# Attention before a mixture of experts: an exponential's low half moved to GpSimd, v's low half in one step, gains spread by a product, a new instruction order

## The chip, the cores and the metric

The kernel runs on one core of one Trainium2 chip. The metric is the device time of one execution in microseconds (us); lower is better. The core has five instruction streams that run side by side and wait for each other through semaphores: TensorE (products into PSUM), VectorE, ScalarE, GpSimd, and SP, which here only issues DMAs. Each executes its own instructions strictly in order.

## The reference

Attention with normalised queries and keys for 8 batches of 12 heads, 448 positions and 64 columns a head, and behind it a layer of 8 experts over the 3584 tokens. Each expert takes 448 tokens, chosen greedily by the logits.

```python
def rmsnorm(x, g):
    rms = np.sqrt(np.mean(x * x, axis=-1, keepdims=True) + 1e-06)
    return x / rms * g
q_n, k_n = (rmsnorm(q, g_q), rmsnorm(k, g_k))
scores = np.matmul(q_n, k_n.transpose(0, 1, 3, 2)) / np.sqrt(q.shape[-1])
attn = np.exp(scores - np.max(scores, axis=-1, keepdims=True))
attn = attn / (np.sum(attn, axis=-1, keepdims=True) + 1e-09)
x = np.matmul(attn, v)                  # then to 3584 tokens of 768
logits = x @ w_gate                     # greedy choice, 448 tokens an expert
for e in range(8):
    out[mask_e] = np.maximum(x[mask_e] @ w1[e], 0.0) @ w2[e]
```

## The kernel before

The kernel keeps single precision by splitting most operands into two 16-bit halves (high and low) and adding three products: high by high, high by low, low by high.

**Tiling.** The 96 heads are worked in 24 groups of four (two pairs). The 448 positions of a pair of heads are seven blocks for each group, so there are 168 blocks d of 128 x 896 scores. Per group: q and k are loaded (lines 222 and 230), squared on ScalarE (`square`), summed on VectorE (`sumsq`, line 286), normalised on GpSimd (k, line 321) and ScalarE (q, line 318), multiplied by `gg` = g_q g_k on GpSimd (`gain`, line 346), split into halves (`hi` on ScalarE, `lo` on GpSimd, lines 351 and 354) and turned by DMA transposes on SP (`transpose`, line 363). For the first two groups (`EARLY`) TensorE does the turning (line 376). Then for each block:

- `max_score` (line 473): a rough product into the one PSUM tile of ring `pm`; `max_reduce` (line 482): VectorE takes the row maxima out of it.
- `scores` (lines 504 and 506): the full product; `exp` (line 512): ScalarE writes the exponentials in single precision.
- `split` (line 528): the low half of an exponential, the full value less its top 16 bits, on GpSimd for the blocks in `LO_POOL` and on VectorE for the others. Blocks in `WIDE` are not split; they are multiplied in single precision (line 547).
- `av` (lines 547 to 557): products with v into a PSUM tile of ring `po` (two buffers).

`MIX` names one of two kinds for every group: nine groups are "4" (blocks 0, 2, 4, 6 wide, low halves of 1, 3, 5 on GpSimd) and fifteen are "2" (blocks 0 and 4 wide; of 1, 2, 3, 5, 6 the low half of block 2 is made by VectorE, the other four by GpSimd). v is loaded into `vraw`, and its halves are made for the position columns that are not wide: `v_hi` on ScalarE (line 440) and `v_lo` on VectorE (line 444). `halves_v` yields the parts: one of 512 columns in a "4" group, two (512 and 256 columns) in a "2" group.

Behind every pair, `x_norm`, `x_hi`, `x_lo` (lines 579 to 602) divide by the sums and write x in halves; line 601 and 602 set the `po` tile free. Per batch (three groups), x is stored (`x_store`, lines 616 and 620), turned by two DMA transposes on SP (`x_dma_turn`, line 609, 24 and 18 blocks) and multiplied by the gate weights (`gate`, lines 658 to 666, into a `po` tile). `Router.early` does the first step of the choice for the first six batches on VectorE.

**Setting up.** `gain_loads` reads g_q and g_k by two DMAs of GpSimd that repeat the row for all 128 partitions (line 143); `gate_loads` reads the gate weights by five DMAs on SP (lines 146 and 150); `gains` multiplies g_q by g_k on VectorE (line 178).

**Order.** Nothing is scheduled while the kernel is built: `plan` lists 2247 tasks, each with its engine, an estimated time (table `US`) and its dependencies, and the string `ORDER` (two characters a task) is the order in which they are issued. `Plan.run` checks that it holds to the dependencies and issues them; each engine then executes its own in that order. The estimates are used for finding such a string only, not when the kernel is built.

After attention the router and the eight experts run (`Router`, `Experts`; lines 864 to 1800), with weights streamed in by SP.

Of the kernel before, what the change touches and what calls it, by code (L numbers as in the profile page):

```python
# [26 lines left out]
F32 = mybir.dt.float32  # L27
# [4 lines left out]
OP = mybir.AluOpType  # L32
# [57 lines left out]
class Attention:  # L90
# [19 lines left out]
    LO_POOL = {"4": (1, 3, 5), "2": (1, 3, 5, 6), "0": (1, 3, 5)}  # L110
    MIX = "444" + 6 * "422" + "222"

    def __init__(self, ctx, tc, q, k, v, g_q, g_k, w_gate, xd, logits, router):
# [13 lines left out]
        gq = c.tile([128, 64], F32, name="gq")  # L127
        gk = c.tile([128, 64], F32, name="gk")
# [31 lines left out]
        def eps():  # L160
            for t in self.sq:
                nc.gpsimd.memset(t[:, :, 64:65], 64e-6)

# [13 lines left out]
        def gains():  # L177
            nc.vector.tensor_tensor(self.gg, gq, gk, op=OP.mult)
# [149 lines left out]
    def engine(self, e, g, a=None):  # L328
        some = self.FIRST[g] if g < len(self.FIRST) else self.TAIL if g >= self.NG - 2 else {}
        return some.get(f"{e}{a}", some.get(e, self.ENG[e]))  # L330
# [99 lines left out]
    def halves_v(self, g):  # L430
# [11 lines left out]
    def v_lo(self, g):  # L442
        for r, h, l in self.halves_v(g):
            self.nc.vector.scalar_tensor_tensor(l, r, self.VS, h, op0=OP.mult, op1=OP.subtract)  # L444
# [159 lines left out]
    def x_dma_turn(self, b, part):  # L604
# [3 lines left out]
        s = slice(24 * part, 24 + 18 * part)  # L608
# [93 lines left out]
    def gate_sum(self, b):  # L702
# [5 lines left out]
    US = dict(small=0.22, rootP=1.19, rootD=0.6, copyA=0.95, sumsq=1.09, normP=1.69, normA=2.1,  # L708
              normD=1.08, gainP=2.09, gainD=1.08, loP=1.89, loD=1.08, turn=1.95, trm=1.16, rows=1.05, loadS=0.66,
              loadA=0.6, loadP=1.0, max=0.2, reduce=1.092, score=0.765, wide=0.248, narrow=0.092,  # L710
              exp=0.917, splitD=1.08, splitP=1.68, xn=0.63, xhi=0.605, xlo=0.68, gate=0.11, early=8.0, xturn=0.4, xtdA0=0.81,
# [4 lines left out]
    def plan(self):  # L716
# [11 lines left out]
        add("gl", "P", 1.32, gain_loads, make="gg32", move=(1.5, 0.4))  # L728
        add("gg", "D", 0.15, gains, after=["gg32"], make="gg")
# [4 lines left out]
        for g in range(self.NG):  # L734
# [18 lines left out]
            else:  # L753
# [25 lines left out]
                for i in range(2):  # L779
                    add("tr" + "hl"[i], "S", US["turn"], self.transpose, g, i, after=[("hl"[i], g, n) for n in "kq"], make=("kq", g, i),  # L780
# [1074 lines left out]
```

## Time and profile before

| | |
|---|---|
| time, median of 3 runs | 998.96 us (994.08 to 999.85) |
| the profiled execution | 998.89 us, span 997.1 us |
| busy in the span: TensorE / VectorE / ScalarE / GpSimd | 92% / 69% / 53% / 43% |
| mean granted TensorE clock | 0.959 of full |
| moved by DMA | 157.78 MB |

The page gives such shares for the whole span; since attention and the experts load the engines differently, the views below are taken by stretches. "L482" is line 482 of the kernel, `out<-in` names the tiles, and an arrow behind idle time names what ended it. TensorE's clock has two levels, 1.2 and 2.4 GHz; a granted clock of 0.50 is the lower.

### The profile page before, as it was taken

To read this page: it belongs to the slowest core of one execution; us is meant where nothing else is said; L and a number is where in the kernel's file an instruction comes from. 1 tells how busy PE (TensorE), PEld (TensorE's weight loads), DVE (VectorE), ACT (ScalarE), POOL (GpSimd) and SP (SyncE) were. 2 spreads that over 40 slices of the span, in tenths; PEclk is the share of its full clock that TensorE was granted. 3 is DMA by queue.
4 is the path that set the end of the run, shared out by engine and by line. 5 is a ranking of instruction groups with operands and counts; after the bars stand their busy time and mean duration, and the time that the engine had idled before them with its cause. 6 is when DMAs were issued, how large, how long until landed. Compare 5 with 4: busy or idle time off the path is not lost.

```text
span 997.1 us, 24885 instructions
## 1 busy us (share of the span) xinstructions
PE 921.2 (92%) x10285; PEld 592.7 (59%) x10286; DVE 691.0 (69%) x1518; ACT 531.8 (53%) x1055; POOL 432.6 (43%) x420
## 2 busy tenths in 40 slices
PE   1889989899899999899869999999999999999996
PEld 1466666666677666667746655556555565555553
DVE  4979998878868788776488777778686758334010
ACT  4879887779778987755405243424242424334111
POOL 5779886877877977854210110311111112020101
PEclk9789999899989999989959999999999999999998
DMA  7286597878889876566236483949493919663101
GB/s 167 79 164 140 128 186 159 190 166 174 173 192 214 157 154 137 112 157 123 69 103 208 141 256 120 278 155 264 146 258 105 300 60 300 220 161 117 40 16 40
DMA packets 263841, 157.78 MB, mean 158 GB/s; under 512 B 189456, under 2 KB 250896, under 8 KB 262704
## 3 DMA queue, kind: packets, MB, share of 16 engines
q1 hardware_dynamic: 258224, 133.65, 55.6%
q0 software_dynamic: 4672, 22.09, 6.6%
q8 instruction: 80, 1.31, 0.5%
q10 hardware_dynamic: 832, 0.46, 0.2%
q14 instruction: 33, 0.27, 0.1%
HBM read 94.49 MB, written 22.02 MB: 117 GB/s over the span
## 4 chain that ended last, share of the span: by engine, by line
issue 33%; PE 16%; POOL 5%; DVE 3%; ACT 1%; POOLq 0%; DVEq 0%; ACTq 0%
PE ph L1638 6%; PE py L1655 3%; POOL out_dram L1671 2%; POOL rows L1576 2%; PE po L547 2%; PE psc L504 2%; PE po L553 1%; PE po L557 1%; PE po L555 1%; PE psc L506 0%; PE rp L1239 0%; PE pm L473 0%; ACT qn L318 0%; DVE vs L444 0%; POOL spacer L1670 0%
## 5 line engine op out<-in xcount | busy, mean ns | idle before, releaser
L482 DVE TENSOR_REDUCE mx<-pm 128x2 f32<-128x896 f32 x162 | 176.2, 1088 | 55.2 <-PE pm L473 54.3
L1638 PE MATMUL ph<-xt,w1h 128*128 128x448 f16 (+2 forms) x804 | 209.7, 344 | 1.0 <-DVE xt L1597 0.5
L547 PE MATMUL po<-v,e 128*128 128x65 f32 (+1 forms) x1056 | 180.0, 285 | 1.6 <-ACT e L512 1.4
L528 POOL TENSOR_TENSOR pl<-e 128x896 f16<-128x896 f32 x87 | 152.0, 1751 | 57.1 <-ACT e L512 56.9
L512 ACT ACTIVATE e<-psc 128x896 f32<-128x896 f32 x168 | 149.1, 912 | 46.6 <-PE psc L506 42.1
L1671 POOL DMA_INDIRECT out_dram<-y,idx x32 | 33.2, 1036 | 311.5 <-ACT y L1657 238.9
L547 PEld LDWEIGHTS po<-v,e 128*128 128x128 f32 (+1 forms) x1056 | 136.9, 182 | 39.3 <-issue 33.7
L1638 PE MATMUL ph<-xt,w1l 128*128 128x448 f16 (+2 forms) x402 | 136.8, 344 | 0.0
L504 PE MATMUL psc<-kq 64*128 64x448 f16 (+1 forms) x1152 | 131.4, 370 | 5.3 <-ACT e L512 4.2
L555 PE MATMUL po<-vs,e 128*128 128x64 f16 (+1 forms) x1008 | 133.3, 197 | 0.0
L553 PE MATMUL po<-vs,e 128*128 128x65 f16 (+1 forms) x1008 | 132.9, 198 | 0.0
L557 PE MATMUL po<-vs,pl 128*128 128x65 f16 (+1 forms) x1008 | 131.9, 196 | 0.0
L1655 PE MATMUL py<-w2h,hh 128*128 128x384 f16 x384 | 125.0, 326 | 0.0
L1655 PE MATMUL py<-w2h,hl 128*128 128x384 f16 x384 | 125.0, 326 | 0.0
L1655 PE MATMUL py<-w2l,hh 128*128 128x384 f16 x384 | 125.0, 325 | 0.0
L1628 ACT ACTIVATE hh<-ph 128x448 f16<-128x448 f32 x64 | 34.8, 543 | 146.4 <-PE ph L1638 129.6
L553 PEld LDWEIGHTS <-e 128*128 128x128 bf16 (+1 forms) x1008 | 112.1, 126 | 0.0
L1638 PEld LDWEIGHTS <-w1h 128*128 128x128 f16 x804 | 74.1, 97 | 61.3 <-issue 1.5
L1655 PEld LDWEIGHTS <-hh 128*128 128x128 f16 x768 | 73.6, 97 | 45.8
L1657 ACT ACTIVATE y<-py 128x384 f32<-128x384 f32 x48 | 23.5, 490 | 133.4 <-PE py L1655 102.2
L557 PEld LDWEIGHTS <-pl 128*128 128x128 f16 (+1 forms) x1008 | 88.7, 103 | 0.0
L1630 DVE SCALAR_TENSOR_TENSOR hl<-ph,hh 128x448 f16<-128x448 f32 x64 | 39.3, 619 | 71.2 <-ACT hh L1628 71.1
(272 smaller groups left out, 1835.3 us busy)
## 6 DMA issues: line engine op xcount, KB each, us to landing
stage<-in_moe_w_dram SPq DMA_DIRECT2D x64, 768.0 KB
vraw<-in_v_dram SPq DMA_DIRECT2D x24, 384.0 KB
xd<-xa SPq DMA_DIRECT2D x8, 1152.0 KB
qkraw<-in_q_dram SPq DMA_DIRECT2D x11, 768.0 KB
qkraw<-in_k_dram SPq DMA_DIRECT2D x11, 768.0 KB
vraw<-in_v_dram SPq DMA_DIRECT2D x48, 32.0 KB
xd<-xa SPq DMA_DIRECT2D x16, 96.0 KB
qkraw<-in_q_dram SPq DMA_DIRECT2D x22, 64.0 KB
```

The lines of the kernel that those rows point to most:

```text
L482: self.nc.vector.tensor_reduce(m, p[r, :, :448], axis=AX.X, op=OP.max)
L504: mm(o, k[r, mine], q[r, all_], start=i == 0, stop=False)
L512: self.nc.scalar.activation(e, p[:, :, :448], AF.Exp, scale=scale)
L528: eng.tensor_tensor(l, self.T["e", d], self.T["ph", d], op=OP.subtract)
L547: nc.tensor.matmul(out, self.T["e", d][:, h, q0:q0 + m], self.v32[g % 2][:, 2 * h + a, wide.index(b % 4)], start=first, stop=last)
L553: nc.tensor.matmul(out, e[:, h, q0:q0 + m], vh, start=first, stop=False)
L555: nc.tensor.matmul(out[:, :64], e[:, h, q0:q0 + m], vl[:, :64], start=False, stop=False)
L557: nc.tensor.matmul(out, l[:, h, q0:q0 + m], vh, start=False, stop=last)
L1630: self.later(0.6, lambda: nc.vector.scalar_tensor_tensor(hl, whole, 0.0, hh, op0=OP.max, op1=OP.subtract), k, 3.5, f)
L1638: nc.tensor.matmul(p, a, b[:, o], start=st, stop=sp)
L1655: nc.tensor.matmul(p, a[:, f, s], b[:, f, o], start=st, stop=sp)
L1671: st = nc.gpsimd.indirect_dma_start(out=self.out, out_offset=bass.IndirectOffsetOnAxis(ap=self.router.idx[k][:n, c:c + 1], axis=0), in_=y[ ...
```

## The change

Five things are changed, all in attention.

1. `LO_POOL["2"]` gains block 2: in the fifteen "2" groups all five low halves are made by GpSimd. VectorE makes none any more.
2. `halves_v` yields one part of all 1024 columns in a "2" group (the wide quarter with them, which nobody reads), so `v_hi` and `v_lo` are one instruction there. A "4" group keeps its one step of 512.
3. g_q and g_k are loaded as single rows, by SP and by ScalarE's queue. VectorE multiplies the rows, a product of TensorE with a row of ones spreads the result over 128 partitions of a `po` tile, and VectorE copies it into `gg`.
4. `x_dma_turn` turns x in four pieces (12, 12, 12 and 6 blocks) in place of two.
5. `ORDER` is another string (2262 tasks). Estimates in `US` and in `plan` that served to find it are changed too.

Read from the two strings: the gate-weight loads are task 6 before and 460 after; `Router.early` is task 2041 of 2247 before and 2189 of 2262 after. SP begins with load 0 of q, the gate weights, loads 2, 1 and 3 of q before; with loads 0, 1, 2 of q, g_q, load 3 of q after. ScalarE's queue begins with four loads of k before; with three, g_k and the fourth after.

```diff
-    LO_POOL = {"4": (1, 3, 5), "2": (1, 3, 5, 6), "0": (1, 3, 5)}
+    LO_POOL = {"4": (1, 3, 5), "2": (1, 2, 3, 5, 6), "0": (1, 3, 5)}
...
-        gq = c.tile([128, 64], F32, name="gq")
-        gk = c.tile([128, 64], F32, name="gk")
+        gq = c.tile([1, 64], F32, name="gq")
+        gk = c.tile([1, 64], F32, name="gk")
+        one = c.tile([1, 128], F32, name="one")
...
-        def gain_loads():
-            for t, src in ((gq, g_q), (gk, g_k)):
-                nc.gpsimd.dma_start(t, bass.AP(tensor=src.tensor, offset=src.offset, ap=[[0, 128], [1, 64]]))
+        def gain_loads(i):
+            eng, t, src = ((nc.sync, gq, g_q), (nc.scalar, gk, g_k))[i]
+            eng.dma_start(t, bass.AP(tensor=src.tensor, offset=src.offset, ap=[[64, 1], [1, 64]]))
...
         def gains():
-            nc.vector.tensor_tensor(self.gg, gq, gk, op=OP.mult)
+            nc.vector.tensor_tensor(gq, gq, gk, op=OP.mult)
+            p = self.po_tile()[:, :64]
+            nc.tensor.matmul(p, one, gq, start=True, stop=True)
+            nc.vector.tensor_copy(self.gg, p)
...
         js = [j for j in range(4) if j not in self.wide_of(g)]
-        for part in (js[:3:2], js[1:2], js[3:]) if len(js) == 3 else (js,):
-            if part:
-                yield self.heads(r, part), *(self.heads(vs[:, i], part)[..., :64] for i in range(2))
+        js = js if len(js) == 2 else [0, 1, 2, 3]
+        if len(js) == 4:
+            yield r, vs[:, 0, :, :64], vs[:, 1, :, :64]
+        else:
+            yield self.heads(r, js), *(self.heads(vs[:, i], js)[..., :64] for i in range(2))
...
-        s = slice(24 * part, 24 + 18 * part)
+        s = slice(12 * part, min(42, 12 * part + 12))
         nc.sync.dma_start_transpose(self.T["xt", b][:, s], self.T["xa", b][:, 128 * s.start:128 * s.stop])
...
-        add("gl", "P", 1.32, gain_loads, make="gg32", move=(1.5, 0.4))
-        add("gg", "D", 0.15, gains, after=["gg32"], make="gg")
+        for i in range(2):
+            add("gl", "SA"[i], 0.6, gain_loads, i, make="gg32", move=(1.5, 0.05))
+        add("gg", "D", 1.0, gains, after=["gg32", ("c", "eps")], make="gg")
...
-                    for i in range(2):
+                    for i in range(4):
...
     ORDER = (
-        "0402000t0m0o07050+03060x0v080u0z0y1009121Q010A0p0n0B111314150C0w1r1O1R0-1N1t161v17191P1S1T181B1D0D1u1s1y1w1+1A"
+        "020u0+00060z0v070809030w0y0n0m0-111312051415160o1710190x1P1O1R1S1Q181T1U1V1X1v1u1s1t1z2L2M1w1A1C1D041x1a1E1F1G"
...
```

## Rows read from the trace of the kernel before

**Rows 1.** Busy time of each engine by stretches of the span. Columns: the stretch and its length, then busy us and instructions of TensorE's products (PE), its weight loads (PEld), VectorE (DVE), ScalarE (ACT) and GpSimd (POOL), the granted TensorE clock as a share of 2.4 GHz, the busy share of the DMA engines, GB/s.

```profile
31.00:495.50 464.50, 429.13 (x6474) 306.97 (x6472) 372.35 (x568) 359.01 (x822) 345.75 (x276) 0.95 0.71 153
75.00:425.00 350.00, 324.17 (x4884) 232.00 (x4882) 293.50 (x429) 286.10 (x663) 285.12 (x228) 0.97 0.77 163
425.00:495.50 70.50, 66.75 (x1214) 51.65 (x1213) 42.33 (x92) 35.90 (x69) 28.73 (x19) 0.95 0.51 122
...
523.00:997.00 474.00, 464.11 (x3481) 269.27 (x3479) 278.55 (x814) 155.45 (x195) 63.47 (x95) 0.99 0.57 168
```

**Rows 2.** Who waited for whom, TensorE alone, 0 to 492 us: us in total, times, longest us.

```profile
PE po L376 <- ACT s L351: 18.6, 3, 16.2
PE pm L473 <- DVE mx L482: 18.1, 16, 2.9
PE po L658 <- DVE xa L602: 4.4, 2, 3.6
...
PE pm L473 <- DMA kq<-s: 1.8, 3, 0.7
```

**Rows 3.** Busy time by short stretches, with the columns of rows 1: the three longest idle gaps of TensorE among those that VectorE ended by lines 482 and 602 from 75 us on, with the stretch at half clock after each; then two shorter gaps, each with the stretch behind it.

```profile
146.57:150.19 3.62, 0.00 (x1) 0.03 (x1) 3.62 (x5) 1.91 (x9) 2.60 (x2) 1.00 0.71 134
151.00:154.40 3.40, 3.30 (x20) 1.31 (x21) 2.53 (x7) 1.52 (x3) 0.07 (x1) 0.50 0.01 2
190.18:193.07 2.89, 0.00 (x1) 0.02 (x2) 2.89 (x4) 0.80 (x1) 2.64 (x6) 0.81 0.96 174
192.00:202.20 10.20, 9.13 (x77) 6.42 (x78) 6.66 (x13) 3.25 (x7) 6.16 (x7) 0.50 0.64 168
265.58:268.28 2.70, 0.00 (x0) 0.00 (x0) 2.70 (x5) 0.68 (x1) 2.70 (x4) 1.00 1.35 203
270.50:280.70 10.20, 10.20 (x101) 7.73 (x102) 5.29 (x9) 5.58 (x11) 4.67 (x3) 0.50 0.54 143
435.17:436.60 1.43, 0.00 (x1) 0.03 (x1) 1.43 (x4) 1.36 (x4) 0.41 (x1) 1.00 0.77 247
437.80:444.50 6.70, 6.70 (x85) 5.24 (x86) 3.04 (x13) 0.92 (x1) 0.62 (x2) 0.50 0.79 272
368.50:369.84 1.34, 0.00 (x1) 0.00 (x1) 1.28 (x2) 1.34 (x7) 1.34 (x1) 1.00 0.33 73
369.84:379.84 10.00, 9.38 (x171) 6.83 (x171) 8.31 (x17) 8.09 (x16) 8.47 (x6) 1.00 0.36 84
```

**Rows 4.** VectorE's timeline in the three gaps. Columns: start us, length us of the merged instructions (xN; x2 is two in a row), engine and line, operation, out<-in; in brackets the idle time before it and what ended that.

```profile
142.77 2.77 DVE L528 TENSOR_TENSOR pl<-e 128x896 f16<-128x896 f32 x1
145.46 3.99 DVE L444 SCALAR_TENSOR_TENSOR vs<-vraw,vs 128x512 f16<-128x512 f32 x2
...
188.03 3.98 DVE L444 SCALAR_TENSOR_TENSOR vs<-vraw,vs 128x512 f16<-128x512 f32 x2
...
262.23 4.40 DVE L444 SCALAR_TENSOR_TENSOR vs<-vraw,vs 128x512 f16<-128x512 f32 x2
```

**Rows 5.** VectorE's timeline at two other places, one step and one pair of line 444.

```profile
285.93 0.69 DVE L444 SCALAR_TENSOR_TENSOR vs<-vraw,vs 128x512 f16<-128x512 f32 x1
...
463.18 1.02 DVE L444 SCALAR_TENSOR_TENSOR vs<-vraw,vs 128x512 f16<-128x512 f32 x2
```

**Rows 6.** GpSimd's timeline in the second gap.

```profile
187.12 2.53 POOL L528 TENSOR_TENSOR pl<-e 128x896 f16<-128x896 f32 x1
```

**Rows 7.** Groups of instructions by line, engine and operation, shapes apart, 0 to 500 us: out<-in with partitions x elements, xcount | busy us, mean ns of one | idle time before and what ended it.

```profile
L528 POOL TENSOR_TENSOR pl<-e 128x896 f16<-128x896 f32 x87 | 152.0, 1751 | 57.1 <-ACT e L512 56.9
...
L444 DVE SCALAR_TENSOR_TENSOR vs<-vraw,vs 128x512 f16<-128x512 f32 x24 | 25.8, 1077 | 0.0
...
L528 DVE TENSOR_TENSOR pl<-e 128x896 f16<-128x896 f32 x15 | 22.5, 1503 | 1.5 <-ACT e L512 1.5
...
L444 DVE SCALAR_TENSOR_TENSOR vs<-vraw,vs 128x256 f16<-128x256 f32 x15 | 16.8, 1121 | 0.0
```

**Rows 8.** The timeline of the first 40 us, all engines, with the columns of rows 4. SPq and ACTq are the queues of SP and ScalarE while they issue a DMA.

```profile
1.75 2.71 SPq L150 DMA_DIRECT2D wg<-in_moe_w_gate_dram  x4
...
8.41 1.25 SPq L222 DMA_DIRECT2D qkraw<-in_q_dram  x2
...
9.67 0.22 DVE L178 TENSOR_TENSOR gg<-gq,gk 128x64 f32<-128x64 f32 x1
...
11.40 1.57 ACT L280 ACTIVATE sq<-qkraw 128x512 f32<-128x512 f32 x3 [9.37 <-DMA qkraw<-in_q_dram]
```

**Rows 9.** The same view of the first microseconds, with the same columns.

```profile
4.00:6.00 2.00, 0.00 (x0) 0.00 (x0) 0.21 (x4) 0.00 (x0) 1.79 (x14) 1.00 1.27 95
...
8.00:10.00 2.00, 0.00 (x0) 0.00 (x0) 0.68 (x3) 0.00 (x0) 0.00 (x0) 1.00 0.09 16
```

**Rows 10.** Instructions of two lines that issue DMA transposes on SP's queue (line 609 for x, 363 for the keys and queries), from their own views: xcount: duration ns min/median/max, first and last start us.

```profile
L609 SPq DMA_TRANSPOSE xt<-xa x14: 2814/3704/5685, 125.9 to 468.1; - x14
...
L363 SPq DMA_TRANSPOSE kq<-s x42: 1302/1599/5276, 66.5 to 450.9; - x42
```

**Rows 11.** VectorE's timeline: the first and the last instruction of Router.early.

```profile
437.76 0.33 DVE L1116 TENSOR_REDUCE best<-logits 128x21 f32<-128x168 f32 x1
...
439.85 0.85 DVE L1156 TENSOR_TENSOR cmp<-key,hit 128x672 bf16<-128x672 f32 x1
```

**Rows 12.** Who waited for whom, VectorE alone, 470 to 495.5 us: us in total, times, longest us.

```profile
DVE z L579 <- PE po L557: 6.4, 4, 3.4
```

More of the change, by code (lines that the diff above doesn't have):

```diff
@@ L162, in eps @@
                 nc.gpsimd.memset(t[:, :, 64:65], 64e-6)
+            nc.gpsimd.memset(one, 1.0)
         def maxima():
@@ L440, in v_hi, with v_lo @@
             self.nc.scalar.activation(h, r, AF.Copy, scale=self.VS)
-    def v_lo(self, g):
-        for r, h, l in self.halves_v(g):
-            self.nc.vector.scalar_tensor_tensor(l, r, self.VS, h, op0=OP.mult, op1=OP.subtract)
+    def v_lo(self, g, n):
+        r, h, l = list(self.halves_v(g))[n]
+        self.nc.vector.scalar_tensor_tensor(l, r, self.VS, h, op0=OP.mult, op1=OP.subtract)
     def v_full(self, g):
@@ L706, in gate_sum @@
         nc.vector.tensor_tensor(L[h:h + 64, m], p[h:h + 64, 3, :8], sc[h:h + 64, 3], op=OP.add)
[L708 to L709 removed]
+    US = dict(small=0.22, rootP=1.19, rootD=0.6, copyA=0.95, sumsq=1.09, normP=1.69, normA=3.45,
+              normD=1.08, gainP=2.09, gainD=1.08, loP=1.89, loD=1.08, turn=1.8, turnl=2.3, trm=1.16, rows=0.6, loadS=0.7,
               loadA=0.6, loadP=1.0, max=0.2, reduce=1.092, score=0.765, wide=0.248, narrow=0.092,
[L711 removed]
+              exp=0.917, splitD=1.08, splitP=1.68, xn=0.63, xhi=0.605, xlo=0.68, gate=0.11, early=3.0, xturn=0.4, xtdA0=0.81,
               xtdA1=0.42, xtdD0=0.55, xtdD1=0.29)
@@ L779, in plan @@
                 for i in range(2):
-                    add("tr" + "hl"[i], "S", US["turn"], self.transpose, g, i, after=[("hl"[i], g, n) for n in "kq"], make=("kq", g, i),
+                    add("tr" + "hl"[i], "S", US[("turn", "turnl")[i]], self.transpose, g, i, after=[("hl"[i], g, n) for n in "kq"], make=("kq", g, i),
                         opens=[("kq", g)] if i == 0 else (), uses=[("s1", g), ("kq", g)], move=(1.5, 2.85))
@@ L788, in plan @@
             n = len(self.wide_of(g))
-            add("vhi", "A", {0: 1.1, 1: 0.94, 2: 0.65}[n], self.v_hi, g, after=[("v", g), *once("v", g)], make=("vh", g),
+            add("vhi", "A", {0: 1.05, 1: 1.05, 2: 0.65}[n], self.v_hi, g, after=[("v", g), *once("v", g)], make=("vh", g),
                 opens=[("V", g)], uses=[("vraw", g)])
@@ L793, in plan @@
                     opens=[("V", g)], uses=[("vraw", g)])
-            add("vlo", "D", {0: 1.23, 1: 1.1, 2: 0.687}[n], self.v_lo, g, after=[("vh", g)], make=("V", g),
-                uses=[("V", g), ("vraw", g)], port=True)
+            for i, part in enumerate(self.halves_v(g)):
+                add("vlo", "D", 0.68 if n == 2 else 1.21, self.v_lo, g, i,
+                    after=[("vh", g)], make=("V", g), uses=[("V", g), ("vraw", g)], port=True)
         count = 0
@@ L853, in plan @@
                 if b < last:
-                    for i in range(2):
-                        add("xtr", "S", 2.5 - 0.3 * i, self.x_dma_turn, b, i, after=x, opens=[("xt", b)] if i == 0 else (),
-                            make=("xt", b, i), uses=[("xb", b), ("xt", b)], move=(1.5, 4.9 - 1.2 * i))
+                    for i in range(4):
+                        add("xtr", "S", 1.9 if i < 3 else 1.2, self.x_dma_turn, b, i, after=x, opens=[("xt", b)] if i == 0 else (),
+                            make=("xt", b, i), uses=[("xb", b), ("xt", b)], move=(1.5, 2.4 if i < 3 else 1.25))
                     for j in range(4):
                         add("gate", "T", 0.33, self.gate, b, j,
-                            after=[*(("xt", b, i) for i in range(2)), "wg"], make=("pg", b), opens=[("gate", b)] if j == 0 else (),
+                            after=[*(("xt", b, i) for i in range(4)), "wg"], make=("pg", b), opens=[("gate", b)] if j == 0 else (),
                             uses=[("xt", b), ("gate", b)], holds=[("po", ("pg", b))] if j == 0 else (), modes=[int(j == 3)] * 2)
```

84 lines of the change are left out of this document (43 added, 41 removed).

## The prediction

> **What bounds the kernel now.** I began with busy time by stretches [rows 1]. Three parts stand out: a fill up to about 31 us, attention from there to 495.5 us, and the experts behind it. From 523 to 997 us TensorE is busy 464 of 474 us; the diff touches no line of that part, so everything must be won or lost before 495.5. In attention no engine but TensorE is near full: between 75 and 425 us it is busy 324 of 350 us (93%), VectorE 294 (84%), ScalarE 286 (82%), GpSimd 285 (81%). From 425 to 495.5 the other three fall to 60% and less while TensorE stays at 95%: it carries a backlog to the end. So time in attention is TensorE's work plus what TensorE loses. The next view says to what it loses: the list of who waited for whom, for TensorE [rows 2]. Behind the fill (18.6 us before its first transposes) its largest wait is the product of the row maxima (line 473) for VectorE's maximum of the product before (line 482), which must empty the one PSUM tile of that ring: 18.1 us in 16 waits. Then comes the gate product for VectorE's line 602, 4.4 us.
>
> Next I looked up the three longest of these waits after 75 us and what came after them [rows 3]. TensorE stands still for 3.62 us from 146.57, 2.89 us from 190.18 and 2.70 us from 265.58, 9.2 us in all, and behind each the granted clock is 0.50 (1.2 GHz in place of 2.4): from 151.0, 192.0 and 270.5, for 3.4, 10.2 and 10.2 us. At half clock half the work is done, so these 23.8 us cost up to 11.9 us more. Which instruction made VectorE late is read from its timeline [rows 4]: v's low half, two steps on line 444, took 3.99, 3.98 and 4.40 us together there, the first time behind a subtraction of an exponential's low half (line 528) of 2.77 us. The same pair took 1.02 us elsewhere, and one step of 512 columns 0.69 [rows 5]. In the same microseconds GpSimd ran a subtraction of its own, stretched to 2.53 us [rows 6]; its mean over all 87 is 1.751 [rows 7]. So steps of VectorE with two SBUF inputs and GpSimd's steps keep each other out for whole instructions, and two steps in a row are kept out twice.
>
> **The change part by part.** The sum is made against the profiled execution: span 997.1, time 998.89, which is the median of the runs (998.96) to 0.1 us.
>
> *Low halves of exponentials.* In the 15 groups of four heads marked "2", one of five subtractions goes from VectorE to GpSimd. VectorE loses 15 instructions of 1.503, 22.5 us; GpSimd gains 15 of 1.751, 26.3 us [rows 7]. What hides GpSimd's part: of 464.5 us it is busy 345.8 [rows 1]. VectorE's part is hidden too, but for the waits of TensorE named above.
>
> *v's low half.* In the same groups two steps (512 and 256 columns) become one over 1024, a quarter of which nobody reads. Free price: 512 columns take 0.69 [rows 5]; a 256-column step adds 0.33 to a pair (1.02 − 0.69), so 512 more columns cost at most 0.66 and the one step 1.2 to 1.35. Free, that is 0.2 to 0.3 us dearer than the pair. (By the same slope a free subtraction of 896 columns comes to about 1.2.) Kept out, it is cheaper: the pair's mean is 1.077 + 1.121 = 2.20 [rows 7], the one step's 1.077 + 0.6 = 1.7. 15 times: −7.5 us of VectorE, with bounds +5 (never kept out) and about −15 (always).
>
> VectorE thus loses some 30 of its 372 us. What of it reaches the end is what TensorE no longer waits. In each of the three stalls one of two lockouts goes; the pair of about 4.0 becomes one step of 1.3 plus one lockout of 1.5 (half of 3.98 − 1.02), 2.8. That takes 1.2 from each, and from the first also the 2.77 − 1.2 = 1.6 of the subtraction before it: 5.2 of the 9.2 us. Gaps of 1.3 to 1.5 us would be left. Such a gap was followed by half clock once (1.43 us at 435.17, then 6.7 us at 0.50) and once not (1.34 us at 368.5, then 1.00) [rows 3], so I take half of the 11.9: 6. Together −11.2, between 0 (the new order puts other stalls in their place) and −21.1 (all gone). Of the other 12.5 us that line 473 waits for line 482 (18.1 less 2.89 and 2.70), in 14 waits, I take a quarter, as VectorE stays the engine that empties the tile: −3, between 0 and −12.5.
>
> *Later lows.* Each moved subtraction ends 1.75 − 1.2, some 0.6 us later, behind a longer queue. TensorE shows no wait for GpSimd now [rows 2]; counted in the two order tables, 20.6 of its tasks lie in the mean between a score and the first product that uses its exponential, and 19.4 in the new order. I take a third of 15 × 0.6: +3, between 0 and the rival below.
>
> *Head: g_q, g_k and the gate weights.* Before, SP issues the five gate-weight loads second (lines 146 and 150), and its next loads of q (line 222) go out at 8.41 only, though the last gate-weight load was issued at 4.46 [rows 8]. The DMA engines are 9% busy from 8 to 10 us [rows 9], and the first square, which waits for q, starts at 11.40. In the new order the gate weights are task 460 in place of 6; SP issues three loads of q and then g_q, ScalarE's queue three of k and then g_k. Behind g_q stands the rest of q on SP, behind g_k the rest of k and ScalarE's squares: a load costs the queue 0.6. The two loads take the gate weights' place, about 1.75, and so go out 6.6 us sooner; but from 4 to 6 us the DMA engines were full, so I take the idle stretch alone. The new product on one row, VectorE's product (0.22) and the copy from PSUM [rows 8] come to about 1 us, in a stretch where VectorE waits for q anyway; if the rows land late, GpSimd's gain starts up to that 1 us later. −4 (8.41 − 4.46), between −6.6 and 0 (the first groups then wait for the later loads).
>
> *Transposes of x in four pieces.* 14 instructions on SP become 28. The 14 took 3.70 in the median; the turn of keys, of 14 blocks, took 1.60 [rows 10]. Pieces of 12, 12, 12 and 6 blocks: 3 × 1.6 + 1.3 = 6.1 against 7.4 for the two. Bounds: 4 × 2.8, the shortest of the old ones, so +3.8 a batch on SP. Queued behind them are loads and turns of keys; of TensorE's waits only 1.8 us are for the turned keys [rows 2]. 0 on the path.
>
> *ScalarE's high half of v:* 768 columns in two steps become 1024 in one, a third more columns and one start less; 0. *Router.early* moves to the last tasks: from its first row to its last it takes 2.9 us of VectorE [rows 11], which waits 6.4 us for line 557 in the last 25 us [rows 12]; 0, and +2.9 without that cover.
>
> Sum: −4 − 11.2 − 3 + 3 = −15.2; 998.9 − 15.2 = 983.7, so **984**. By the bounds of the terms, 959 to 1002.
>
> **Rivals.** *A, all stalls of this kind go:* −6.6 − 21.1 − 12.5 = −40, **959**. For it: no subtraction of line 528 is left on VectorE, so the clusters of two and three locked-out steps can't form. Against it: one step can still be locked out for 1.5 us, and a new order has new places for it.
>
> *B, the offload gives nothing back:* GpSimd works 26 us longer and keeps VectorE's remaining two-input steps out that much more; each of the 24 steps on line 444 could lose the 1.5 us of one lockout, 36 us, more than the 30 won. Then only the head is left: **995**. For it: in [rows 4, 5] three of the pairs shown are locked out and one is not, so a lockout is no rare thing. Against it: there are 24 such steps where there were 39 and 15 subtractions. The Trainium skill (Perfetto Trace Analysis, Optimizing Scalar/DVE Operations) warns of just this: VectorE and GpSimd share an SBUF port, so moving work between the two may not help. The stretched rows agree that they exclude each other; whether the move helps no row of before can show.
>
> *C, GpSimd becomes the bound; slower:* between 75 and 425 us it gets 350/464.5 of the 15 subtractions, 11.3 × 1.751 = 19.8 us, so 304.9. If it can't be busier than its 81% of now, because it waits for ScalarE's exponentials as before, the stretch takes 304.9/0.815 = 374 us, 24 longer, and with the head the time is **1019**. It decides from the point where lows come later than TensorE's 20 tasks of slack. For it: at my forecast it would be busy 305 of 335 us, 91%, near TensorE's own 93%. Against it: it loses lockouts too, and TensorE shows that 93% can be held.
>
> **How the numbers follow.** Forecast 0.48, A 0.12, B 0.24, C 0.16. A measurement of this kernel tells about 1% from no change, 989 to 1009. The likeliest case's own range is 974 to 993 (its terms at half and at one and a half of what I took, and 2 us for the runs); I put nine tenths of it under 989 (0.43), and with A 0.12 and 0.01 of B that makes faster 0.56. The rest of both and B: same 0.28. C: slower 0.16. The range for 8 in 10 takes in A's figure to within 1 us and B's spread up to 1004 and leaves C out: 960 to 1004.
>
> **What would show it.** Right: 102 subtractions on GpSimd and none on VectorE; line 444 24 times at a mean under 1.9; the first square before 8 us; TensorE's wait of line 473 for line 482 under 13 us; fewer than 30 us at half clock before 495 us (the head has some of its own); attention's end near 480. Wrong: a line of TensorE waiting for line 528 on GpSimd (C); line 444 over 2.2 in the mean with waits of line 473 as before (B); new stalls over 2.5 us elsewhere, each with half clock behind it, since the order is new everywhere and I can price only the stalls that I see.

## The result and the profile after

The changed kernel takes 968.73 us in the median of 4 runs (964.25 to 969.87); the kernel before took 997.98 beside it. The ratio is 0.9704, 95% interval 0.9659 to 0.9748: faster by 3%, inside the range of 960 to 1004, and twice the forecast's gain (29 us where 15 were forecast). The profiled execution is the fastest of the four, 964.25 us (span 962.5), so the two profiles lie 34.6 us apart, some 5 more than the medians. The whole gain lies in attention: it ends at 460.9 us in place of 495.5, and what follows takes 501.6 us in both (997.1 − 495.5 and 962.5 − 460.9). Times here and below are medians of all runs of a kernel; without the slow runs among them e11's is 964.25, e13's 998.35, and that of the kernel before beside e1 to e4 994.64 us.

Busy time by stretches of the kernel after, with the columns of [rows 1]:

```profile
31.00:460.90 429.90, 412.09 (x6472) 295.85 (x6470) 349.75 (x540) 355.69 (x797) 364.25 (x284) 0.99 0.80 161
75.00:425.00 350.00, 341.81 (x5422) 247.40 (x5422) 290.99 (x433) 300.36 (x669) 315.29 (x244) 0.99 0.89 177
425.00:460.90 35.90, 33.48 (x675) 26.94 (x674) 19.63 (x48) 17.64 (x34) 16.02 (x12) 1.00 0.36 99
```

Multiply TensorE's busy time by the granted clock: 412.09 × 0.99 = 408 us after, 429.13 × 0.95 = 408 us before [rows 1], about the same work, in 6472 and 6474 products. Before, it took 464.5 us: TensorE was busy for 429.1, some 21 of them lost to the lower clock, and idle for 35.4. After, it takes 429.9, with 412.1 us busy and 17.8 idle. So the 34.6 us are in equal parts 17.0 less busy time for as many products, most of it clock, and 17.6 less idle time. VectorE's busy time fell from 372.35 to 349.75, 22.6 us, but its share of the stretch hardly moved: 0.802 before, 0.814 after. GpSimd rose to 90% between 75 and 425 us.

The clock column misses one stretch. In the kernel after it shows 1.00 up to 41.9 us, yet six products of one size take 1.30 us there and 0.74 a little later:

```profile
31.00:41.90 10.90, 8.95 (x50) 3.52 (x48) 10.01 (x13) 8.81 (x27) 7.60 (x9) 1.00 0.20 37
...
39.96 1.30 PE L512 MATMUL psc<-kq 64*128 64x448 f16 x6 [0.18 <-DVE mx L490]
45.31 0.74 PE L512 MATMUL psc<-kq 64*128 64x448 f16 x6 [0.32 <-DVE mx L490]
```

By these durations TensorE ran at half clock there too, which cost up to half of its 8.95 busy us: with it the clock lost some 8.5 us after where it lost 21 before, so some 13 of the 17.0 are clock. All kernels of the new order begin so, up to 37 us in e14 and to 41 to 45 in the others; in the kernel before such products take 0.74 from 32.6 us on. Below, kernels are therefore compared within one order by TensorE's busy time for the same products, beside the column.

TensorE's waits in the kernel after, 0 to 470 us, with the columns of [rows 2]:

```profile
PE po L182 <- DVE gq L180: 7.4, 1, 7.4
PE pm L481 <- DVE mx L490: 7.1, 8, 2.5
PE po L382 <- ACT s L357: 4.8, 1, 4.8
```

The wait for the row maxima (18.1 us in 16 [rows 2]) is 7.1 us in 8, and no wait for line 536, GpSimd's subtraction, appears. Short stretches after, as in [rows 3]: three gaps of TensorE, the first and the last with the stretch at half clock behind it, the middle one with the stretch behind it.

```profile
46.20:48.66 2.46, 0.05 (x2) 0.00 (x0) 1.43 (x3) 1.80 (x3) 1.86 (x2) 1.00 0.47 79
48.70:52.10 3.40, 3.25 (x18) 1.21 (x18) 3.37 (x3) 2.25 (x4) 1.81 (x1) 0.51 1.20 290
...
135.00:136.60 1.60, 0.04 (x4) 0.06 (x1) 1.60 (x4) 1.54 (x5) 1.52 (x1) 1.00 0.80 160
136.60:143.00 6.40, 6.37 (x109) 3.88 (x109) 6.37 (x10) 4.77 (x10) 5.37 (x3) 1.00 1.11 247
...
247.90:249.50 1.60, 0.05 (x2) 0.04 (x1) 1.60 (x4) 0.00 (x0) 1.60 (x2) 1.00 0.18 36
250.10:256.90 6.80, 6.80 (x63) 4.65 (x61) 1.92 (x5) 3.53 (x10) 4.73 (x4) 0.50 1.01 304
```

These are the only two stretches that the column shows at half clock between 31 us and attention's end, 10.2 us; [rows 3] alone hold 30.5. The groups that answer to [rows 7]:

```profile
L536 POOL TENSOR_TENSOR pl<-e 128x896 f16<-128x896 f32 x102 | 175.6, 1729 | 29.5 <-ACT e L520 23.3 <-DVE z L589 2.3 <-DMA xd<-xa 2.1
...
L452 DVE SCALAR_TENSOR_TENSOR vs<-vraw,vs 128x1024 f16<-128x1024 f32 x15 | 25.2, 1677 | 0.0
L452 DVE SCALAR_TENSOR_TENSOR vs<-vraw,vs 128x512 f16<-128x512 f32 x9 | 16.0, 1775 | 0.0
```

All 102 subtractions are on GpSimd, each no longer than before. v's low half takes 41.2 us in 24 steps, where it took 42.6 in 39. A step of 512 columns, 1.077 us in [rows 7], now takes 1.775, no less than one of 1024; with 0.69 for a free one [rows 5], more than half of that is time kept out. The head, from the timeline as in [rows 8], with the first exponential:

```profile
5.21 1.15 ACT L285 ACTIVATE sq<-qkraw 128x512 f32<-128x512 f32 x2 [3.19 <-DMA qkraw<-in_q_dram]
...
7.08 0.20 DVE L180 TENSOR_TENSOR gq<-gq,gk 1x64 f32<-1x64 f32 x1
7.43 0.65 PE L182 MATMUL po<-gq,one 1*128 1x64 f32 x2 [7.43 <-DVE gq L180]
8.12 0.22 DVE L183 COPY gg<-po 128x64 f32<-128x64 f32 x1 [0.84 <-PE po L182]
...
35.36 0.92 ACT L520 ACTIVATE e<-psc 128x896 f32<-128x896 f32 x1 [0.71 <-PE psc L514]
```

The kernel before:

```profile
32.23 0.92 ACT L512 ACTIVATE e<-psc 128x896 f32<-128x896 f32 x1 [0.52 <-PE psc L506]
```

The first square comes 6.2 us sooner (5.21 for 11.40), yet the first exponential comes 3.1 us later (35.36 for 32.23).

### The profile page after: what moved, and what is told of

Same layout as the page of the kernel before. It is cut to its first block, busy times and chain, and to the rows that moved or that the text cites. A ratio compares the mean times of both kernels' runs of the same rounds, so it can differ in the third digit from the quotient of the medians.

```text
span 962.5 us, 24853 instructions
## 1 busy us (share of the span) xinstructions
PE 905.3 (94%) x10287; PEld 582.3 (61%) x10288; DVE 674.1 (70%) x1489; ACT 534.5 (56%) x1040; POOL 454.4 (47%) x434
## 4 chain that ended last, share of the span: by engine, by line
PE 41%; issue 35%; DVE 9%; DMA 6%; POOL 6%; ACT 2%; SPq 0%; POOLq 0%; DVEq 0%; ACTq 0%
PE po L555 9%; PE psc L512 8%; PE ph L1649 6%; PE pm L481 3%; DMA kq<-s 3%; PE py L1666 3%; DVE mx L490 3%; POOL rows L1587 3%; PE psc L514 2%; POOL out_dram L1682 2%; PE po L561 2%; PE po L565 2%; PE po L563 2%; DMA mt<-qm 1%; DVE vs L452 1%
## 5 line engine op out<-in xcount | busy, mean ns | idle before, releaser
L490 DVE TENSOR_REDUCE mx<-pm 128x2 f32<-128x896 f32 x162 | 176.0, 1086 | 45.9 <-PE pm L481 44.9
L536 POOL TENSOR_TENSOR pl<-e 128x896 f16<-128x896 f32 x102 | 175.6, 1729 | 29.5 <-ACT e L520 23.3
L555 PE MATMUL po<-v,e 128*128 128x65 f32 (+1 forms) x1056 | 173.8, 280 | 0.3 <-DVE z L587 0.2
L555 PEld LDWEIGHTS po<-v,e 128*128 128x128 f32 (+1 forms) x1056 | 132.7, 177 | 33.6 <-issue 31.1
L563 PE MATMUL po<-vs,e 128*128 128x64 f16 (+1 forms) x1008 | 130.5, 194 | 0.2 <-DVE vs L452 0.2
L512 PE MATMUL psc<-kq 64*128 64x448 f16 (+1 forms) x1152 | 127.6, 359 | 2.4 <-DVE mx L490 1.5
L561 PE MATMUL po<-vs,e 128*128 128x65 f16 (+1 forms) x1008 | 129.8, 195 | 0.0
L565 PE MATMUL po<-vs,pl 128*128 128x65 f16 (+1 forms) x1008 | 129.1, 194 | 0.0
L1639 ACT ACTIVATE hh<-ph 128x448 f16<-128x448 f32 x64 | 34.8, 543 | 143.4 <-PE ph L1649 140.3
L561 PEld LDWEIGHTS <-e 128*128 128x128 bf16 (+1 forms) x1008 | 109.1, 123 | 0.0
L1666 PEld LDWEIGHTS <-hh 128*128 128x128 f16 x768 | 73.6, 97 | 45.8
```

Source lines behind the costliest of these rows:

```text
L490: self.nc.vector.tensor_reduce(m, p[r, :, :448], axis=AX.X, op=OP.max)
L512: mm(o, k[r, mine], q[r, all_], start=i == 0, stop=False)
L536: eng.tensor_tensor(l, self.T["e", d], self.T["ph", d], op=OP.subtract)
L555: nc.tensor.matmul(out, self.T["e", d][:, h, q0:q0 + m], self.v32[g % 2][:, 2 * h + a, wide.index(b % 4)], start=first, stop=last)
L561: nc.tensor.matmul(out, e[:, h, q0:q0 + m], vh, start=first, stop=False)
L563: nc.tensor.matmul(out[:, :64], e[:, h, q0:q0 + m], vl[:, :64], start=False, stop=False)
```

## The experiments

"Old order" is the kernel before with one thing changed, "new order" the changed kernel with one thing undone or added. Kernels of one group ran beside the same runs of the kernel before: 995.52 (the first four), 997.16, 997.24, 995.35 and 999.46 us (the last two). These scatter by 4 us, so a difference of that size between kernels of different groups shows little.

### Which part does it

Only the low halves of block 2, in the old order:

```diff
-    LO_POOL = {"4": (1, 3, 5), "2": (1, 3, 5, 6), "0": (1, 3, 5)}
+    LO_POOL = {"4": (1, 3, 5), "2": (1, 2, 3, 5, 6), "0": (1, 3, 5)}
```

> The kernel before with one part alone: block 2's low half of an exponential on GpSimd in the fifteen '2' groups, in the old order. Theory 1 (the relief of VectorE ends the stalls, whatever the order): 6 to 12 us under the kernel before, line 473's wait for line 482 under 14 us. Theory 2 (the new order is what pays, the parts alone nothing): within 4 us of the kernel before, or slower, as GpSimd's 26 us were not planned for.

977.44, ratio 0.9819 (0.9755 to 0.9884): −18 us by one tuple, without the new order, and more than the 6 to 12 that theory 1 gave. The stretch from 31 us to attention's end and its middle, as in [rows 1], the one stretch at half clock after 75 us, and TensorE's waits for VectorE from 75 us on:

```profile
31.00:476.50 445.50, 414.64 (x6472) 298.05 (x6468) 356.38 (x552) 359.34 (x822) 364.78 (x291) 0.98 0.75 160
75.00:425.00 350.00, 328.93 (x5126) 236.12 (x5124) 294.96 (x440) 295.51 (x681) 308.37 (x245) 1.00 0.81 171
334.80:338.20 3.40, 3.40 (x26) 1.02 (x26) 2.12 (x3) 2.16 (x5) 3.04 (x6) 0.50 1.17 271
```

```profile
PE pm L473 <- DVE mx L482: 9.3, 14, 1.5
PE po L658 <- DVE xa L602: 1.1, 1, 1.1
```

The granted clock rose from 0.95 to 0.98 and VectorE's share is 0.800. The stretch is 19.0 us shorter: TensorE is idle for 30.9 us in place of 35.4, 4.5 less, and busy for 414.64 in place of 429.13, 14.5 less for the same products. So most of this gain is clock. The longest of the waits shown is 1.5 us where it was 3.62, and of the 30.5 us at half clock in [rows 3] none is left, while 3.4 stand at a new place. The pair of steps of v's low half is still there and takes 45.8 us in all, more than the 42.6 before, so by itself it is not what cost the 18 us. The same with `halves_v` of the change (v in one step):

> The kernel before with both parts of the change on the halves (lows on GpSimd, v's low half and high half in one step each), in the old order. Theory 1: 14 to 18 us under the kernel before, fewer than 25 us at half clock before attention's end. Theory 2: within 5 us of the kernel before.

976.87: one step of v shows no gain over e1 in this order, though line 446 takes 33.5 us here in place of e1's 45.8. Then the reverse edit of e1 in the new order:

> The changed kernel with fifteen lows given back to VectorE, in the new order. Theory 1: 8 to 14 us over the changed kernel. Theory 2: under 5 us over it.

1005.38, ratio 1.0095 (1.0058 to 1.0131). The new order without the move is slower than the kernel before; the move is worth 36.7 us there, far more than the 8 to 14 of theory 1. VectorE's groups and the stretch to attention's end:

```profile
L536 DVE TENSOR_TENSOR pl<-e 128x896 f16<-128x896 f32 x15 | 28.1, 1873 | 10.5 <-ACT e L520 10.5
```

```profile
31.00:504.90 473.90, 434.49 (x6474) 308.97 (x6473) 377.29 (x554) 357.68 (x797) 342.50 (x268) 0.94 0.70 146
```

The fifteen take 28.1 us and VectorE stands 10.5 us before them, waiting for the exponential (1.5 us before [rows 7]): the new order places them where VectorE has to wait. e4 undoes the one step of v as well:

> The changed kernel with both parts on the halves undone (fifteen lows on VectorE, v's halves in two steps in those groups), so the new order, the head and the four pieces of x alone. Theory 1: 14 to 20 us over the changed kernel, with stalls and half clock behind pairs of v's low half again. Theory 2: under 6 us over it, so some 24 us under the kernel before.

1008.72 (ratio 1.0044 to 1.0193 at 95%): no better. The new order pays only together with the move.

### The small parts

e5 puts only the gate-weight loads of the old order late (task 6 goes ahead of the first turn of x); e6 puts them second on SP in the new one:

```diff
-        "020u0+00060z0v070809030w0y0n0m0-
+        "020u0p0+00060z0v070809030w0y0n0m0-
```

> The kernel before with two tasks of its order moved: the gate-weight loads from sixth place to just ahead of the first transposes of x, and VectorE's work on them to just ahead of the first gate product. If the head is worth what its microseconds are (first square 4 to 6 us sooner): 4 to 6 us under the kernel before. If attention's pace is set behind the fill: within 2 us of it.

> The changed kernel with the gate-weight loads moved back to SP's second place, nothing else. Head worth its microseconds: first square near 11 us and 4 to 6 us over the changed kernel. Not worth them: within 2 us.

996.25 beside 997.16, and 969.43 beside the changed kernel's 968.73: nothing in either. The first squares and first exponentials, e5 and then e6:

```profile
9.04 0.63 ACT L280 ACTIVATE sq<-qkraw 128x512 f32<-128x512 f32 x1 [7.01 <-DMA qkraw<-in_q_dram]
30.62 0.92 ACT L512 ACTIVATE e<-psc 128x896 f32<-128x896 f32 x1 [0.87 <-PE psc L506]
...
7.83 1.15 ACT L285 ACTIVATE sq<-qkraw 128x512 f32<-128x512 f32 x2 [5.80 <-DMA qkraw<-in_q_dram]
37.98 0.92 ACT L520 ACTIVATE e<-psc 128x896 f32<-128x896 f32 x1 [0.71 <-PE psc L514]
```

The edits moved the first square by 2.4 and 2.6 us only, not by the 4 to 6 expected, and the first exponential by 1.6 and 2.6 the same way; the end did not follow. The other half of the head, g_q and g_k as rows and their spreading by a product, was not undone in any run. e7 takes v in two steps in the new order (`halves_v` of before):

> The changed kernel with v's halves in two steps in the fifteen '2' groups again. One step saves lockouts (theory 1): 4 to 8 us over the changed kernel, the pair's mean over 2.5 us. One step saves nothing, since line 452 takes 41 us in all after as line 444 took 42.6 before: within 3 us.

973.5 (967.15 to 976.3), 4.8 us over the changed kernel's 968.73 (964.25 to 969.87): the one step may be worth some 5 us in the new order, but the runs overlap, and it is 0.6 in the old. e8 turns x in two pieces again:

```diff
-        s = slice(12 * part, min(42, 12 * part + 12))
+        if part % 2:
+            return
+        s = slice(12 * part, (24, 0, 42)[part])
```

> The changed kernel with x turned in two DMA transposes of 24 and 18 blocks, issued where the first and the third piece stand. If the pieces are off the path, as predicted: within 3 us of the changed kernel. If shorter pieces let SP's loads and turns of keys through in time: 4 us or more over it, and a wait of TensorE for the turned keys above the 2.1 us of the changed kernel.

971.61 (967.51 to 978.72), 2.9 us over the changed kernel and within the spread of its own runs: no clear effect.

### Is it VectorE's time, the lockouts, or the use of the result?

A filler on VectorE in place of each moved subtraction: an unused maximum over the exponential, one input. GpSimd does not keep it out (1034 to 1086 ns in e9), nor does it keep GpSimd out (line 529 of e9 takes 1716 ns in the mean, as in e1).

```diff
+        if self.MIX[d // 7] == "2" and d % 7 == 2:
+            self.nc.vector.tensor_reduce(self.spare, self.T["e", d], axis=AX.X, op=OP.max)
```

> The kernel of e1 (fifteen lows on GpSimd, old order) and, where VectorE made each of these lows, a maximum over the same 896 exponentials that nobody uses: one SBUF input, some 1.0 to 1.1 us, of a kind (as the sums of squares) that the traces never show stretched. VectorE so keeps the free length of the work that was moved, but no lockout by GpSimd and none of GpSimd. Lockouts are the cause (theory 1): within 5 us of e1, so about 980. VectorE's time is the cause (rival): most of e1's 18 us is lost, 990 to 997.

> The changed kernel with the same unused maximum behind each of the fifteen moved lows. Lockouts are the cause of the 36 us that giving the lows back cost: within 6 us of the changed kernel. VectorE's time is the cause: 20 us or more over it.

991.96 and 985.7: 16 us of VectorE without a lockout cost 14.5 us over e1 and 17 over the changed kernel. In the new order VectorE also waits 10.3 us for the exponential in front of the fillers (1.4 in the old), so there a part of the cost may come from the place and not from the length. Two fillers at each place, in the old and in the new order:

> The kernel before with the fifteen low halves on GpSimd (977.4), and in their place two unused maxima on VectorE instead of one: some 32 us of VectorE that lock nothing out, where one maximum each (16.0 us) gave 992.0 and the lows themselves (22.5 us) 997. If VectorE's time alone sets the cost, at 14.5 / 16.0 = 0.9 us for each us, the time is 977.4 + 29 = 1006. If the first us cost most and the rest is hidden, or if lockouts are what costs, it stays under 997.

> The changed kernel with two unused maxima on VectorE at each of the fifteen places in place of one. One gave 985.7, 17 over the changed kernel, 1.05 us for each of 16.2 us. If VectorE's time alone sets the cost: 968.7 + 34 = 1003, near the 1005.4 that the low halves on VectorE gave with 28.1 us. If those cost more because they lock GpSimd out and are locked out: under 997.

999.06 and 1005.59: the whole of the gain is gone in both, by 32 us of VectorE that lock out nobody. In the old order that is 21.6 us for 32.3, 0.7 for each, less than the 0.9 of one filler and between the two theories. TensorE's wait for the row maxima rises with the fillers: 12.1 us in e1, 17.5 in e9 and 20.1 in e13; 7.1 in the changed kernel, 22.8 in e10 and 33.8 in e14. The groups of e14 and its stretch to attention's end:

```profile
L540 DVE TENSOR_REDUCE spare<-e 128x2 f32<-128x896 f32 x15 | 16.3, 1086 | 0.5
L539 DVE TENSOR_REDUCE spare<-e 128x2 f32<-128x896 f32 x15 | 16.2, 1081 | 10.4 <-ACT e L521 10.4
```

```profile
31.00:499.70 468.70, 427.63 (x6472) 305.57 (x6470) 381.09 (x570) 357.19 (x797) 363.58 (x284) 0.95 0.71 148
```

Clock and VectorE's share are near those of the kernel before again: 0.95 and 0.813. Then the subtraction itself as a filler: GpSimd makes all 102, and VectorE makes block 2's once more into a tile that nobody reads.

> The changed kernel, GpSimd making all 102 low halves, and VectorE making the fifteen of block 2 once more into a tile that nobody reads: the subtraction's own time and lockouts, but no product that uses it. With the low halves used from VectorE and not made by GpSimd the time was 1005.4; with an unused maximum of 1.07 us it was 985.7. If it is VectorE's time with its lockouts (1.5 to 1.9 us each, 22 to 28 us): 993 to 1000. If what cost in 1005.4 was that the product waited for a low half made on VectorE: no more than the maximum, 986. If lockouts cost GpSimd too, whose work is 26 us more here: 1005 or over.

> The same in the old order: the kernel before with the fifteen low halves on GpSimd (977.4) and the same subtractions once more on VectorE, unused. VectorE's time with its lockouts (some 22.5 us as before): 977.4 + 20 = 997, the time of the kernel before. If GpSimd's 26 us more with these lockouts cost as well: over 1005. If only the use of a low half made on VectorE cost: 977 to 992.

1009.71 and 1008.43, at least as slow as with the results used (1005.38 in e3, 995.35 in the kernel before beside e16). So what costs is not the use of a low half made on VectorE; both times are those that the last branch gave, in which the lockouts cost GpSimd too. In e15:

```profile
L539 DVE TENSOR_TENSOR spare<-e 128x896 f16<-128x896 f32 x15 | 28.2, 1879 | 10.6 <-ACT e L521 10.6
```

```profile
L537 POOL TENSOR_TENSOR pl<-e 128x896 f16<-128x896 f32 x102 | 187.5, 1847 | 42.4 <-ACT e L521 42.3
```

41 us are lost for 28.2 us of VectorE, against 37 for 32.5 us of maxima; in e16, 31 us for 25.9, against 21.6 for 32.3. At the rate of the maxima the time alone would cost 32 and 17 us. The other 9 and 14 go with the lockouts, in which GpSimd's subtractions get longer too (1847 ns in the mean for 1729, and 1778 for 1716 in e16): in the old order nearly as much as the time itself.

### Is GpSimd's longer work hidden, and where does it end?

e11 and e12 leave the fifteen low halves out on both engines (a tile of zeros takes their place).

> The changed kernel with the fifteen moved lows made by no engine: their product takes a tile of zeros, so that part of the result is left out, and all other work is the same. GpSimd's 26 us are hidden (its 90% between 75 and 425 us is no bound): within 4 us of the changed kernel. GpSimd paces attention by now: 8 to 20 us under it.

> The kernel before with the same fifteen lows made by no engine (zeros in their product). If what counts is that VectorE is rid of them: as e1, within 5 us of 977. If GpSimd's extra work costs in the old order too: 8 us or more under e1.

964.89 in the new order: GpSimd's 26 us cost about 4 us, no more than the runs scatter. e15 has the same 26 us more than e3 and is 4 us slower; in the old order e16 has them more than the kernel before and is 13 slower, so there, with VectorE's subtractions still in place, they are not hidden. In the old order e12 takes 984.31, 7 us more than e1, which does more work. The table below shows where: TensorE's idle time is the same (31.2 and 30.9 us), its busy time 4.6 us longer, so it is the clock, granted at 0.97 in place of 0.98. Why it fell more often no run shows. e17 and e18 leave out v's low half (lines 452 and 444), all of it, on the changed kernel and on e1.

```diff
     def v_lo(self, g, n):
+        return
```

> The changed kernel without line 452: v's low half is zero, so its product adds nothing; TensorE's products, GpSimd and the order are as in the changed kernel. VectorE loses 41 of its 350 us in attention. Its share of the stretch from 31 us to attention's end was 0.80 to 0.82 in the kernel before, the changed one and with fillers, and the stretch followed VectorE's work. TensorE's products need 408 us at full clock (412.09 us busy at a granted 0.99) of the 429.9 us. If VectorE sets the pace until TensorE is full, the stretch falls to 412 to 422 us: 952 to 961 us. If the changed kernel is already bound by TensorE or by another wait, it stays at 966 to 971.

> The kernel before with the fifteen low halves on GpSimd (977.4) and without line 444: v's low half is zero. VectorE loses 45 of its 356 us. With 10 us less of VectorE by v's one step, or with neither engine making the low halves, the old order did not get under 977. If the old order has a floor of its own there, its waits not VectorE's: 972 to 980. If those two runs only scattered and VectorE sets the pace here too: 950 to 965.

962.82 and 969.15: e17 between what the two theories gave, e18 just under the 972 of a floor and over the other's 965. VectorE's busy time fell by 28.0 and 37.6 us only, not by the 41 and 45 expected, because small steps of the router got longer: line 1137, a TENSOR_SCALAR of 128x21 integers, takes 1.66 us in e17 and 0.17 as line 1135 of the kernel after. The stretches to attention's end, e17 and then e18:

```profile
31.00:458.90 427.90, 410.57 (x6479) 294.41 (x6477) 321.77 (x518) 355.67 (x799) 352.80 (x285) 0.99 0.80 162
```

```profile
31.00:465.10 434.10, 411.82 (x6472) 296.16 (x6468) 318.79 (x512) 358.14 (x821) 356.28 (x290) 0.99 0.77 164
```

The same view of the kernels whose VectorE work differs, in order of that work, in us from 31 to attention's end (one profiled execution each; the time is the median of the runs):

| kernel | VectorE busy | TensorE busy | TensorE idle | length | VectorE's share | time |
|---|---|---|---|---|---|---|
| new order, v's low half left out (e17) | 321.8 | 410.6 | 17.3 | 427.9 | 0.75 | 962.8 |
| **after** | 349.8 | 412.1 | 17.8 | 429.9 | 0.81 | 968.7 |
| new order, x in two pieces (e8) | 355.3 | 418.6 | 22.4 | 441.0 | 0.81 | 971.6 |
| new order, gate weights early (e6) | 355.4 | 412.3 | 18.3 | 430.6 | 0.83 | 969.4 |
| new order, v in two steps (e7) | 361.2 | 417.6 | 23.4 | 441.0 | 0.82 | 973.5 |
| new order, one filler (e10) | 367.9 | 425.6 | 29.1 | 454.7 | 0.81 | 985.7 |
| new order, lows back (e3) | 377.3 | 434.5 | 39.4 | 473.9 | 0.80 | 1005.4 |
| new order, two fillers (e14) | 381.1 | 427.6 | 41.1 | 468.7 | 0.81 | 1005.6 |
| new order, unused lows (e15) | 383.3 | 432.0 | 45.8 | 477.8 | 0.80 | 1009.7 |
| old order, v's low half left out (e18) | 318.8 | 411.8 | 22.3 | 434.1 | 0.73 | 969.2 |
| old order, both parts (e2) | 346.5 | 413.8 | 28.0 | 441.8 | 0.78 | 976.9 |
| old order, lows left out (e12) | 349.4 | 419.3 | 31.2 | 450.4 | 0.78 | 984.3 |
| old order, lows on GpSimd (e1) | 356.4 | 414.6 | 30.9 | 445.5 | 0.80 | 977.4 |
| old order, one filler (e9) | 369.1 | 418.5 | 34.0 | 452.5 | 0.82 | 992.0 |
| **before** | 372.4 | 429.1 | 35.4 | 464.5 | 0.80 | 998.0 |
| old order, two fillers (e13) | 380.1 | 432.6 | 34.8 | 467.4 | 0.81 | 999.1 |
| old order, unused lows (e16) | 380.6 | 432.3 | 40.4 | 472.7 | 0.81 | 1008.4 |

In the new order the time rises by 36.9 us for 31.3 of VectorE from the kernel after up to e14 (1.2 for each) and falls by only 5.9 for 28.0 below it (0.2); in the old one it is 21.6 for 23.7 above e1 (0.9) and 8.3 for 37.6 below it (0.2). So the slope changes somewhere near 350 to 360 us of VectorE's work. One execution each does not say where: e6 and e8 have the same work and lengths 10 us apart, and e12 lies off the line. TensorE's columns show by what way VectorE's work costs: from e1 to e13 its idle time rises by 3.9 us and its busy time, for the same products, by 18.0, which is clock; from the kernel after to e14 by 23.3 and 15.5. No run holds the clock fixed, so what the gaps cost alone is not shown. The kernel before stood where VectorE's time is dear; the change takes it to where TensorE is busy 412.09 of 429.9 us (96%), and leaving out v's low half on top (e17) wins only 5.9 us more.

## Why the prediction was half right

*The bound.* "No engine but TensorE is near full" is the sentence that misled. 93% busy counts work at half clock as full work: at full clock TensorE had 408 us of work in 464.5, 88%. VectorE's share stayed between 0.78 and 0.83 in every kernel of the table with 346 us of VectorE's work or more, and above some 350 to 360 us its time counted about one for one. Why the share is not 1 no experiment shows. A part is the half clock itself: in the four such stretches of [rows 3] VectorE is busy 17.5 of 30.5 us and TensorE 29.3. For the rest, in the kernel after line 490 still waits 44.9 us in 61 times for the product of line 481; the two engines hand one PSUM tile to and fro, and a second one was not tried.

*The step that failed* is "What of it reaches the end is what TensorE no longer waits", and in it above all the clock. The sum took −8.2 us of idle time (5.2 of the three stalls, 3 of the other waits) and −6 of clock, half of what the half clock behind the three stalls cost. The move alone (e1) gave −4.5 of idle time and −14.5 of clock. The stalls shrank as forecast, to 1.5 us and less, but the half clock went behind all of them, and so did that behind the gap at 435.17, for which the sum had no term. In the new order the move (e3 against after) took away 21.6 us of idle time and 22.4 of busy time, in a profiled pair that lies 44 us apart where the medians lie 36.7. That VectorE's time drives both, and not the lockouts alone, show the fillers, which cause no lockout and take the gain away (e13, e14). So the price of VectorE's 22.5 us was not the part of three visible stalls that they lengthen but near their whole length and more: 18 us in the old order, 36.7 in the new.

Of the signs under "Right" those of the mechanism came true (102 subtractions on GpSimd, line 452 24 times at a mean of 1.72 us, the wait for the row maxima at 7.1 us), while attention ended at 460.9 us and not near 480: they showed the direction and not the size. That the time lies inside the range of 960 to 1004 is owed to the range's width. The sum of the terms' bounds, 959 to 1002, leaves out the +3.8 a batch of x in pieces and the +2.9 of *Router.early*.

*v's low half.* The term was −7.5 us of VectorE with bounds of +5 and −15; it came to −1.4 (42.6 to 41.2), as 24 steps are kept out at 1.68 and 1.78 us in the mean. In time the one step gave some 5 us in the new order (e7, not clear of the runs) and 0.6 in the old (e2 against e1).

*Head.* The step was right (first square before 8 us), and its price of −4 is not borne out: the gate weights' part, 2.4 and 2.6 us of the first square and 1.6 and 2.6 of the first exponential, changed the end by −0.9 and +0.7, which is 0 within the runs (e5, e6). In the kernel after the first exponential came 3.1 us later in spite of the earlier square; what in the new fill delayed it is open.

*Later lows* (+3): the 26 us of GpSimd cost about 4 us in the new order (e11), so the term stands within the runs, and *C* falls: GpSimd is busy 315.29 of 350 us and TensorE never waits for line 536. C's point, that GpSimd could not be busier than 81%, did not hold: its waits for the exponentials fell from 56.9 us [rows 7] to 23.3. *x in four pieces* at 0 holds within the runs.

*B* falls in its result and holds in its mechanism: each remaining step of line 452 is kept out more, yet the offload gave 18 to 36.7 us. The Trainium skill (Perfetto Trace Analysis, Optimizing Scalar/DVE Operations) says that handing work to GpSimd may make sense where VectorE is saturated, and that moving work between the two might not help; here it did with VectorE at 80%, since fifteen steps of 1.50 us left an engine whose time counted and arrived at 1.73 us on one whose time cost about 4 (e11). *A*'s 959 was the nearest of the figures, by all stalls gone with all of their clock, and as to the clock it was right; e17, with all of v's low half gone too, shows 962.8.

*The order* was priced at nothing, with only a warning that it is new everywhere. Together with the new head and the four pieces it costs some 10 us without the move (e3 against before) and is worth some 8 with it (976.9 in e2, 968.7 after), a gain of which no term of the sum spoke. The order alone was not run.

Open: why the clock fell more often in the old order without any of the fifteen low halves (e12, 984.3) than with them on GpSimd. Its waits of line 475 for VectorE are 13.1 us in 14, about e1's 12.1 in 15.

## What to carry to other kernels

Multiply TensorE's busy time by its granted clock before you call it the bound: a mean clock of 0.95 made 429 busy us 408, 88% of the stretch. An engine that is busy 80% of the time can still be worth a microsecond for each of its own; a filler of known length on it (15 instructions of 1.07 us, e9 and e10) shows in one run what that is, and leaving work out shows where it ends. Split each difference into TensorE's idle time and its busy time for the same products: the second is clock, and a list of the longest waits does not price it. Here a move off VectorE gave 0.8 (e1, 18 for 22.5) to 1.3 us (e3, 36.7 for 28.1) for each microsecond moved, not the part of the longest stalls that names it.

## What was not expected of the hardware

Of TensorE's loss in the kernel before, 35.4 us was idle time and some 21 clock, and the clock gave the greater part of e1's gain. In e1, 16 us of VectorE's busy time less raised the mean granted clock from 0.95 to 0.98, and two fillers (e14) brought it back to 0.95 from the 0.99 of the changed kernel. After a gap of 1.60 us at 247.9 the clock stood at 0.50 for 6.8 us, after one of 1.60 us at 135.0 it stayed at 1.00; the gap's length alone does not tell.

One-input maxima ran beside GpSimd without being stretched (1.07 to 1.09 us in the mean in e9, e10 and e14), while the two-input subtraction of the same size took 1.50 in the kernel before, 1.87 in e3 and 1.88 in e15. The Trainium skill (SBUF — State Buffer, Terms) calls the port pair of the two engines an exclusive lock held for the whole instruction; the stretched two-input steps agree, and the maxima show that not every VectorE instruction takes part. The number of inputs alone does not tell: the router's one-input step of 128x21 integers took 0.17 us in the kernel after and 1.66 in e17, where it began at 440.4 beside a subtraction of GpSimd from 440.3 to 442.1.
